# Side work queued behind the latest gate in a fused delta-rule attention and two-stage MoE kernel, with independent list scatters

## The chip, the cores and the metric

The kernel runs on one core of one Trainium2 chip. Its engines are TensorE (PE, matrix products), VectorE (DVE), ScalarE (ACT), GpSimd (POOL) and SyncE (SP, which issues most DMAs). Each engine takes its instructions strictly in the order in which the program queues them, and an instruction that waits holds all behind it on its engine. The metric is the device time of the core in microseconds (us), the median of several runs.

## What is computed

The input is q, k and v (4 batches, 8 heads, 768 positions, 48 columns) and a factor beta for each position. Three computations follow each other: a delta-rule attention, a gated feed-forward layer over the 3072 tokens with 384 columns, and a routed layer with 8 experts that gives each token to the expert with the largest logit.

```python
k_n = k / (np.linalg.norm(k, axis=-1, keepdims=True) + 1e-06)
for t in range(S):                                     # attention
    y[:, :, t] = np.einsum('bhd,bhde->bhe', q[:, :, t], state)
    v_old = np.einsum('bhde,bhd->bhe', state, kt)
    state = state + bt * np.einsum('bhd,bhe->bhde', kt, vt - v_old)
...
xn = x / rms * rms_g                                   # feed-forward
g = xn @ w_gate
x = (g / (1 + np.exp(-g)) * (xn @ w_val)) @ w_out
...
e_idx = np.argmax(x @ w_gate2, axis=1)                 # routed layer
for e in range(8):
    mask = e_idx == e
    out[mask] = gate_w * sigmoid(x @ w_og)[:, e] * (np.maximum(x[mask] @ w1[e], 0) @ w2[e])
```

(In the code of the reference the three stand as functions; the names are shortened here.)

## The kernel before

**Stages.** The sequence is cut into 6 chunks of 128 positions, m = 0 to 5, and each chunk into two groups of two batches, g = 0 and 1; (m,g) has 256 tokens. For each chunk the attention part runs `early(m)` (squares and norms of the keys with the powers nrm on GpSimd at L129, Gram products, and `solve`, the inverse of a triangular matrix in many small VectorE operations from L260 to L294, then a corner step on TensorE at L312 and L315), and for each (m,g) `late(m, g)`: a chain z (TensorE, L335), v (VectorE, L339), u (TensorE, L342), right (ScalarE, L346), y (TensorE, L357), x (ScalarE, L362), s (TensorE, L368), right (VectorE, L371), where the last hands the state to the next half. Then `scale` (L616: bss, ri, x) and `turn` (L635: the transposes xt, with xh and xl) make the operands of the feed-forward.

**The block.** `block(m, g)` (L656) is the feed-forward of one (m,g), and it is run for all 12 of them in order. It has 12 steps, called gates here and counted through the kernel from 1. One gate is 18 matmuls gv into one of two PSUM buffers (L670), tanh th and a copy of the value val on ScalarE (L676, L678), the gate multiplication on VectorE (L679), th times val on GpSimd (L681), and h with its low part on ScalarE and GpSimd (L683, L684). Two gates later TensorE multiplies h into po (L694). th and val have two buffers, h has three. "Block (1,0)" is the feed-forward of chunk 1, group 0, whose gates start with number 25.

**Weights.** The 36 pieces of the feed-forward weights come as raw tiles of 64-bit floats and are converted by hand (L508 to L614): a copy on ScalarE (L548), three steps of bit work on VectorE (L550, L551, L554), and a high and a low part on ScalarE and VectorE or GpSimd (L570, L571). The last 11 pieces share four attention buffers, so the load of one has to wait for the conversion of the one four before it.

**Routing.** After each (m,g) the router (L720 to L791) writes the numbers of its tokens into the lists of the eight experts, with two scatters of 128 tokens each, an indirect DMA that GpSimd issues (L787). The routed layer reads the lists at the end.

**The order of the work.** The class `Weave` mixes the block, as main line, with side generators: weights, lengths, early, late, scale, route and grams. Each `yield` names the TensorE time of its step and a gap until the next one, and a scheduler of the framework then orders the instructions of each engine by priority and expected times within the dependences. `issue_after(ins)` puts all instructions of a step that follow on the same engine behind ins. Before, only `solve` of chunks above 0 used it (`Attn.behind` with `M.gate`, the latest gate multiplication).

## Time and profile before

| | us |
|---|---|
| median of 3 runs | 1089.02 |
| lowest and highest run | 1082.79, 1089.41 |
| profiled execution | 1088.74 |
| its span | 1086.9 |

The trace holds each instruction's start, length, engine, source line and tiles, and for idle time what ended it. The granted clock is that of TensorE, as a share of full speed. A stretch of 100 us in which TensorE is busy for 97 has hardly any place where another engine can cost something. The trace groups instructions that follow one another into one row with a count (x4).

### The profile page before, as it was taken

To read this page: it belongs to the slowest core of one execution; us is meant where nothing else is said; L and a number is where in the kernel's file an instruction comes from. 1 tells how busy PE (TensorE), PEld (TensorE's weight loads), DVE (VectorE), ACT (ScalarE), POOL (GpSimd) and SP (SyncE) were. 2 spreads that over 40 slices of the span, in tenths; PEclk is the share of its full clock that TensorE was granted. 3 is DMA by queue.
4 is the path that set the end of the run, shared out by engine and by line. 5 is a ranking of instruction groups with operands and counts; after the bars stand their busy time and mean duration, and the time that the engine had idled before them with its cause. 6 is when DMAs were issued, how large, how long until landed. Compare 5 with 4: busy or idle time off the path is not lost.

```text
span 1086.9 us, 27674 instructions
## 1 busy us (share of the span) xinstructions
PE 976.6 (90%) x11189; PEld 918.0 (84%) x11189; DVE 698.4 (64%) x1976; ACT 474.9 (44%) x1241; POOL 460.8 (42%) x526
## 2 busy tenths in 40 slices
PE   3725888989999989999999999998998989999993
PEld 2725787889988989899989989998998989999993
DVE  5996889849963977279936975244328645557550
ACT  6625552354345434533354334434344534455440
POOL 9608343453444344444454333437533543312110
PEclk9999899999999999899999989999999999999997
DMA  9811770122212131221122120003205574345320
GB/s 290 230 59 43 220 141 1 31 75 60 45 31 64 51 65 31 46 60 45 37 70 60 31 45 17 2 17 146 73 1 167 189 249 161 111 178 200 125 87 15
DMA packets 55433, 97.05 MB, mean 89 GB/s; under 512 B 6400, under 2 KB 41878, under 8 KB 52482
## 3 DMA queue, kind: packets, MB, share of 16 engines
q1 hardware_dynamic: 45266, 48.76, 17.1%
q0 software_dynamic: 7680, 45.08, 11.9%
q8 instruction: 90, 1.47, 0.6%
q10 hardware_dynamic: 2352, 1.37, 0.5%
q14 instruction: 45, 0.37, 0.2%
HBM read 83.78 MB, written 12.09 MB: 88 GB/s over the span
## 4 chain that ended last, share of the span: by engine, by line
PE 42%; DVE 17%; issue 15%; POOL 11%; DMA 8%; ACT 5%; POOLq 0%; SPq 0%; ACTq 0%; DVEq 0%
PE gv L670 14%; PE cpo L1053 8%; PE ph L1032 7%; PE po L694 7%; DVE tmp L275 3%; POOL th L681 3%; DVE x L279 3%; POOL h L684 2%; PE y L357 2%; DVE ng L294 1%; DMA raw<-in_wv_dram 1%; POOL raw L558 1%; DMA sq<-in_kv_dram 1%; ACT h L683 1%; DVE th L679 1%
## 5 line engine op out<-in xcount | busy, mean ns | idle before, releaser
L681 POOL TENSOR_TENSOR th<-th,val 128x256 f32<-128x256 f32 x144 | 114.1, 793 | 218.7 <-DVE th L679 191.9
L694 PE MATMUL po<-wout,h 128*128 128x400 f32 x864 | 192.1, 354 | 5.5 <-ACT h L683 4.1
L683 ACT ACTIVATE h<-th 128x256 fp32r<-128x256 f32 x144 | 60.1, 417 | 231.4 <-POOL th L681 231.0
L694 PEld LDWEIGHTS po<-wout,h 128*128 128x128 f32 x864 | 148.5, 189 | 10.5 <-ACT h L683 5.3
L670 PE MATMUL gv<-xh,wl 128*128 128x256 f32 x864 | 149.2, 291 | 3.6 <-DVE th L679 3.4
L670 PE MATMUL gv<-xh,wgv 128*128 128x256 f32 x864 | 149.1, 293 | 2.5 <-DVE th L679 2.1
L679 DVE SCALAR_TENSOR_TENSOR th<-th,gv 128x256 f32<-128x256 f32 x144 | 59.8, 416 | 137.9 <-ACT val L678 134.2
L684 POOL TENSOR_TENSOR h<-th,h 128x256 fp32r<-128x256 f32 x144 | 109.5, 761 | 74.6 <-ACT h L683 74.3
L670 PEld LDWEIGHTS gv<-xh,wl 128*128 128x128 f32 x864 | 126.0, 194 | 8.1 <-DVE th L679 6.1
L670 PEld LDWEIGHTS gv<-xh,wgv 128*128 128x128 f32 x864 | 124.2, 195 | 6.3 <-DVE th L679 3.3
L1053 PE MATMUL cpo<-w2h,ch 128*128 128x384 f32 (+1 forms) x464 | 124.5, 341 | 4.6 <-ACT w2h L993 3.6
L275 DVE TENSOR_TENSOR tmp<-nb,x 128x110 f32<-128x110 f32 (+35 forms) x366 | 106.3, 330 | 3.9
L279 DVE TENSOR_TENSOR x<-x,tmp 128x110 f32<-128x110 f32 (+35 forms) x366 | 102.4, 317 | 0.2
L1032 PE MATMUL ph<-xT,w1h 128*128 128x256 f32 (+4 forms) x528 | 95.4, 315 | 0.4 <-DVE ch L1037 0.3
L1053 PEld LDWEIGHTS cpo<-w2h,ch 128*128 128x128 f32 (+1 forms) x464 | 82.0, 184 | 7.3 <-ACT w2h L993 4.3
L676 ACT ACTIVATE th<-gv 128x256 f32<-128x256 f32 x144 | 54.5, 379 | 76.9 <-PE gv L670 69.1
L1032 PEld LDWEIGHTS ph<-xT,w1h 128*128 128x128 f32 x528 | 82.9, 192 | 1.8 <-DVE ch L1037 0.6
L670 PE MATMUL gv<-xl,wgv 128*128 128x256 f32 x432 | 78.5, 288 | 0.3 <-DVE xl L651 0.2
L1053 PE MATMUL cpo<-w2l,ch 128*128 128x384 f32 (+1 forms) x232 | 78.0, 337 | 0.0
L670 PE MATMUL gv<-xl,wl 128*128 128x256 f32 x432 | 77.3, 287 | 0.0
L1037 DVE SCALAR_TENSOR_TENSOR ch<-ph,ch 128x512 fp32r<-128x512 f32 (+4 forms) x64 | 39.1, 611 | 42.8 <-ACT ch L1036 42.8
L670 PEld LDWEIGHTS gv<-xl,wgv 128*128 128x128 f32 x432 | 64.0, 195 | 1.1 <-DVE xl L651 0.7
(241 smaller groups left out, 1765.3 us busy)
## 6 DMA issues: line engine op xcount, KB each, us to landing
kT<-in_kqT_dram SPq DMA_DIRECT2D x24, 192.0 KB, 3.5
raw<-in_wo_dram SPq DMA_DIRECT2D x12, 384.0 KB, 8.0
left<-in_kqT_dram SPq DMA_DIRECT2D x24, 192.0 KB, 4.3
v<-in_kv_dram SPq DMA_DIRECT2D x12, 384.0 KB, 3.6
raw<-in_wg_dram SPq DMA_DIRECT2D x12, 384.0 KB, 3.8
raw<-in_wv_dram SPq DMA_DIRECT2D x12, 384.0 KB, 4.3
sq<-in_kv_dram SPq DMA_DIRECT2D x10, 384.0 KB, 3.5
ek<-in_kqT_dram SPq DMA_DIRECT2D x18, 192.0 KB, 3.4
```

The source lines that it names most:

```text
L275: nc.vector.tensor_tensor(out=t, in0=nb[:, k + 1:, k:k + 1].to_broadcast([P, n, b - a]), in1=x[:, k:k + 1, a:b].to_broadcast([P, n, b - a] ...
L279: nc.vector.tensor_tensor(out=x[:, k + 1:, a:b], in0=x[:, k + 1:, a:b], in1=t, op=ALU.add)
L670: nc.tensor.matmul(out=ps[:, gv], lhsT=self.weight(wi, cc, gv, slice(f * P, f * P + P)), rhs=xx[:, cc], start=i == 0, stop=i == 8)
L676: nc.scalar.activation(out=th, in_=ps[:, 0], func=AF.Tanh, scale=0.5)
L679: self.gate = nc.vector.scalar_tensor_tensor(out=th, in0=th, scalar=1.0, in1=ps[:, 0], op0=ALU.add, op1=ALU.mult).ins
L681: nc.gpsimd.tensor_tensor(out=th, in0=th, in1=val, op=ALU.mult)
L683: nc.scalar.activation(out=h2[:, 0], in_=th, func=AF.Copy)
L684: nc.gpsimd.tensor_tensor(out=h2[:, 1], in0=th, in1=h2[:, 0].bitcast(F32), op=ALU.subtract)
L694: nc.tensor.matmul(out=po[t], lhsT=h[:, ts], rhs=self.wo[wi][:, f], start=f == 0 and i == 0, stop=f == 11 and i == 2)
L1032: nc.tensor.matmul(out=ph[:, fl], lhsT=w1[wi][:, cc, f * P:(f + 1) * P], rhs=xt[:, xi, cc], start=i == 0, stop=i == 8)
L1037: nc.vector.scalar_tensor_tensor(out=hl, in0=ph, scalar=0.0, in1=hh.bitcast(F32), op0=ALU.max, op1=ALU.subtract)
L1053: nc.tensor.matmul(out=po[t][0:rows[t]], lhsT=hs[f // 2][:, hi, f % 2, t * P:t * P + rows[t]], rhs=w2[wi][:, f], start=f == 0 and i == 0, ...
```

## The change

1. The class Attn loses `due` and `behind`: the solve is no longer put behind the gate by that means.
2. `block` keeps in `evict` the latest copy of the value (ScalarE, L678) and the latest gate multiplication (VectorE, L679). `Weave.step` puts every step of every side generator behind both: all side work of ScalarE and VectorE emitted after a gate stands behind that gate's two instructions. Before the first gate `evict` is empty, and it is emptied ahead of each unit of the routed layer.
3. The list scatters are declared independent of each other, as they write slots of different tokens. The gather that reads the lists still waits for all.

```diff
-        self.due = lambda: None
...
-    def behind(self, m):
-        due = self.due() if m else None
-        return nullcontext() if due is None else self.tc.issue_after(due)
...
-        solve = self.solve(m)
-        while True:
-            with self.behind(m):
-                t = next(solve, None)
-            if t is None:
-                break
+        for t in self.solve(m):
...
-        self.ready, self.fetched, self.gate = -1, False, None
+        self.ready, self.fetched = -1, False
+        self.evict = []
...
-            nc.scalar.activation(out=val, in_=ps[:, 1], func=AF.Copy)
-            self.gate = nc.vector.scalar_tensor_tensor(out=th, in0=th, scalar=1.0, in1=ps[:, 0], op0=ALU.add,
-                                                       op1=ALU.mult).ins
+            i = nc.scalar.activation(out=val, in_=ps[:, 1], func=AF.Copy)
+            j = nc.vector.scalar_tensor_tensor(out=th, in0=th, scalar=1.0, in1=ps[:, 0], op0=ALU.add, op1=ALU.mult)
+            self.evict = [i.ins, j.ins]
...
-            nc.gpsimd.indirect_dma_start(
+            i = nc.gpsimd.indirect_dma_start(
...
-                bounds_check=NE * NT - 1, oob_is_err=False)
+                bounds_check=NE * NT - 1, oob_is_err=False).ins
+            self.tc.declare_no_dep(i, group="list", reason="slots of other tokens")
+            self.tc.add_to_no_dep_group("list", i)
...
     def step(self, side):
-        try:
-            pe, gap = next(side[0])
-        except StopIteration:
-            self.sides.remove(side)
-            return
+        with ExitStack() as st:
+            for ins in self.first():
+                st.enter_context(self.tc.issue_after(ins))
+            try:
+                pe, gap = next(side[0])
+            except StopIteration:
+                self.sides.remove(side)
+                return
...
-    A.due = lambda: M.gate
+    W.first = lambda: M.evict
...
+        M.evict = []
         W.run(C.unit(u, xg[u], xt[u], p2, new, after, next_unit, u + 1 == len(subs)))
```

No instruction is added or removed on TensorE, VectorE, ScalarE or GpSimd; what moves is their order. Line numbers after the change are some ten lower (L679 is L670, L787 is L778, L260 is L258, L275 is L273, L279 is L277, L371 is L369, L632 is L623, L129 is L127, L339 is L337).

The first place is VectorE at the first gate, whose gate multiplication writes th_1365 (raw tiles are weight pieces in conversion, nrm, n, aT and naT are norms of chunk 1, v is the chain of chunk 0). Before:

```order
L554 SCALAR_TENSOR_TENSOR raw_1610<-raw_1610 128x384
L138 RECIPROCAL n_1418<-n_1418 128x32
L551 SCALAR_TENSOR_TENSOR raw_1569<-raw_1569 128x384
L571 TENSOR_TENSOR wgv_82<-raw_1124,wgv_81 128x384
L139 TENSOR_TENSOR n_1418<-n_1418,beta 128x32
L554 SCALAR_TENSOR_TENSOR raw_1569<-raw_1569 128x384
L141 STREAM_TRANSPOSE aT_1422<-n_1418 128x32
L571 TENSOR_TENSOR wl_1607<-raw_1550,wl_1607 128x384
L143 TENSOR_SCALAR naT_1424<-aT_1422 128x32
L679 SCALAR_TENSOR_TENSOR th_1365<-th_1365,gv_1278 128x256
```

And now:

```order
L369 TENSOR_TENSOR right_78<-right_78,s_1052 48x8x48 x2
L545 SCALAR_TENSOR_TENSOR raw_1124<-raw_1124 128x384
L369 TENSOR_TENSOR right_79<-right_79,s_1085 48x8x48 x2
L562 TENSOR_TENSOR wgv_82<-raw_1124,wgv_81 128x384
L337 TENSOR_TENSOR v_0_802<-v_0_802,z_1104 128x4x48
L337 TENSOR_TENSOR v_0_802<-v_0_802,z_1105 128x4x48
L670 SCALAR_TENSOR_TENSOR th_1365<-th_1365,gv_1278 128x256
L541 TENSOR_SCALAR raw_1217<-raw_1217 128x384
L541 TENSOR_SCALAR raw_1399<-raw_1399 128x384
L133 TENSOR_SCALAR nrm_1232<-nrm_1232 128x32
L541 TENSOR_SCALAR raw_1407<-raw_1407 128x384
```

The conversions of the later pieces and the norms of chunk 1 stand behind the first gate now; the gate itself moved from row 229 of VectorE's order to row 177. The first transpose of the solve of chunk 1 (L260) moved from behind the fifth gate to behind the ninth, and the first of the transposes at its end (L288) from behind gate 16 to behind gate 21.

The second place is VectorE at the 24th gate (th_3099), the last of block (0,1), with the scale of (1,0) (bss_3024 and x_2582) and the solve of chunk 2 (tmp and x_3003). Before:

```order
L279 TENSOR_TENSOR x_3003<-x_3003,tmp_2_3042 128x29x2
L371 TENSOR_TENSOR right_78<-right_78,s_2984 48x8x48 x2
L625 TENSOR_SCALAR bss_3024<-bss_3024 128x2
L245 TENSOR_TENSOR left_77<-gq_3068,maskU 64x4x128 x2
L632 SCALAR_TENSOR_TENSOR x_2582<-x_2582,ri_3088,rmsg 128x384 x2
L679 SCALAR_TENSOR_TENSOR th_3099<-th_3099,gv_3047 128x256
L275 TENSOR_TENSOR tmp_3_3108<-nb_2927,x_3003 128x56 x2
```

And now, 41 rows behind that gate:

```order
L277 TENSOR_TENSOR x_3003<-x_3003,tmp_8_3202 128x23x5
L273 TENSOR_TENSOR tmp_9_3253<-nb_2927,x_3003 128x110 x2
L277 TENSOR_TENSOR x_3003<-x_3003,tmp_9_3253 128x22x5 x2
L369 TENSOR_TENSOR right_78<-right_78,s_2984 48x8x48 x2
L273 TENSOR_TENSOR tmp_10_3258<-nb_2927,x_3003 128x105
L616 TENSOR_SCALAR bss_3024<-bss_3024 128x2
L716 TENSOR_SCALAR y_3235<-po_2147 128x384
L273 TENSOR_TENSOR tmp_10_3258<-nb_2927,x_3003 128x126
L277 TENSOR_TENSOR x_3003<-x_3003,tmp_10_3258 128x21x5
L277 TENSOR_TENSOR x_3003<-x_3003,tmp_10_3258 128x21x6
L623 SCALAR_TENSOR_TENSOR x_2582<-x_2582,ri_3088,rmsg 128x384 x2
```

The scale of (1,0) stood ahead of the 24th gate and of the rows of the solve from tmp_3 on; now it stands behind the gate and behind tmp_0 to tmp_10.

The third place is GpSimd at gates 39 to 42, with the two scatters of the routing of pos_4436 and the powers nrm of chunk 3. Before:

```order
L681 TENSOR_TENSOR th_4173<-th_4173,val_4175 128x256
L787 DMA list<-tok,pos_4436 25600x1
L684 TENSOR_TENSOR h_4179<-th_4173,h_4179 128x256
L787 DMA list<-tok,pos_4436 25600x1
L681 TENSOR_TENSOR th_4255<-th_4255,val_4257 128x256
L684 TENSOR_TENSOR h_4261<-th_4255,h_4261 128x256
L681 TENSOR_TENSOR th_4336<-th_4336,val_4338 128x256
L684 TENSOR_TENSOR h_4342<-th_4336,h_4342 128x256
L129 TENSOR_TENSOR nrm_4349<-ss_4348,half 128x8 x2
L681 TENSOR_TENSOR th_4460<-th_4460,val_4462 128x256
```

And now:

```order
L672 TENSOR_TENSOR th_4173<-th_4173,val_4175 128x256
L675 TENSOR_TENSOR h_4179<-th_4173,h_4179 128x256
L672 TENSOR_TENSOR th_4255<-th_4255,val_4257 128x256
L675 TENSOR_TENSOR h_4261<-th_4255,h_4261 128x256
L672 TENSOR_TENSOR th_4336<-th_4336,val_4338 128x256
L127 TENSOR_TENSOR nrm_4349<-ss_4348,half 128x8
L675 TENSOR_TENSOR h_4342<-th_4336,h_4342 128x256
L778 DMA list<-tok,pos_4436 25600x1 x2
L127 TENSOR_TENSOR nrm_4349<-ss_4348,half 128x8 x3
L672 TENSOR_TENSOR th_4460<-th_4460,val_4462 128x256
```

The scatters moved two gates later and stand side by side; the four powers, of which two stood four gates earlier, stand around them. At gates 64 and 88 four powers stand directly ahead of the pair.

## Rows read from the trace of the kernel before

**Rows 1.** The head of the page: span, and busy time of TensorE.

```profile
span 1086.9 us, 27674 instructions
...
PE 976.6 (90%) x11189; PEld 918.0 (84%) x11189; DVE 698.4 (64%) x1976; ACT 474.9 (44%) x1241; POOL 460.8 (42%) x526
```

**Rows 2.** Windows: start:end, length, busy per engine (instructions), clock, DMA share, GB/s.

```profile
100.00:150.00 50.00, 45.32 (x600) 40.96 (x598) 41.62 (x85) 33.93 (x88) 23.05 (x20) 0.90 0.80 199
...
250.00:350.00 100.00, 97.32 (x1386) 89.59 (x1386) 69.92 (x225) 43.23 (x121) 43.96 (x52) 1.00 0.19 45
```

**Rows 3.** Windows of the solve of chunk 1 and the chain behind it.

```profile
158.60:206.70 48.10, 43.67 (x290) 40.02 (x290) 45.32 (x168) 14.04 (x43) 20.33 (x25) 0.96 0.04 9
206.70:254.50 47.80, 43.05 (x898) 39.96 (x899) 28.74 (x60) 24.73 (x64) 22.25 (x23) 0.96 0.27 69
```

**Rows 4.** The list of waits: who waited for whom, us in total, times, longest.

```profile
POOL list L787 <- DMA list<-tok,pos: 24.5, 8, 4.6
...
PE y L357 <- ACT right L346: 10.9, 8, 2.6
```

**Rows 5.** Timeline of GpSimd: start, us, line, operation, count [idle before <-what ended it].

```profile
440.09 1.06 POOL L787 DMA_INDIRECT list<-tok,pos  x1 [0.17 <-issue]
445.77 0.98 POOL L787 DMA_INDIRECT list<-tok,pos  x1 [4.62 <-DMA list<-tok,pos]
446.76 0.77 POOL L681 TENSOR_TENSOR th<-th,val 128x256 f32<-128x256 f32 x1
447.46 3.29 POOL L129 TENSOR_TENSOR nrm<-ss,half 128x8 f32<-128x8 f32 x2
```

**Rows 6.** Timeline of VectorE at the first gates.

```profile
132.49 0.42 DVE L679 SCALAR_TENSOR_TENSOR th<-th,gv 128x256 f32<-128x256 f32 x1 [1.45 <-ACT val L678]
...
138.07 1.09 DVE L551 SCALAR_TENSOR_TENSOR raw<-raw 128x384 int32<-128x384 int32 x1
```

**Rows 7.** Timeline of VectorE from the solve of chunk 1 to the scale.

```profile
158.61 2.07 DVE L260 STREAM_TRANSPOSE nb<-xr 128x1024 f32<-128x1024 f32 x1
...
173.11 0.41 DVE L679 SCALAR_TENSOR_TENSOR th<-th,gv 128x256 f32<-128x256 f32 x1
...
204.84 1.99 DVE L288 STREAM_TRANSPOSE ng<-xa 128x1024 f32<-128x1024 f32 x1
...
237.20 0.57 DVE L339 TENSOR_TENSOR v<-v,z 128x192 f32<-128x192 f32 x2
...
242.98 0.20 DVE L275 TENSOR_TENSOR tmp<-nb,x 128x31 f32<-128x31 f32 x1
...
246.78 1.11 DVE L371 TENSOR_TENSOR right<-right,s 48x384 f32<-48x384 f32 x2
```

**Rows 8.** Timeline of TensorE: first matmul of the first block and of block (1,0).

```profile
119.76 1.65 PE L670 MATMUL gv<-xh,wgv 128*128 128x256 f32 x6
...
254.53 0.88 PE L670 MATMUL gv<-xh,wgv 128*128 128x256 f32 x6
```

**Rows 9.** Timeline of TensorE: the five y that waited behind a list scatter.

```profile
396.31 0.32 PE L357 MATMUL y<-right,left 128*64 128x48 f32 x2 [2.62 <-ACT right L346]
...
451.00 1.02 PE L357 MATMUL y<-right,left 128*64 128x48 f32 x8 [2.13 <-ACT right L346]
...
567.68 1.54 PE L357 MATMUL y<-right,left 128*64 128x48 f32 x17 [1.05 <-ACT right L346]
...
630.86 0.45 PE L357 MATMUL y<-right,left 128*64 128x48 f32 x2 [2.63 <-ACT right L346]
...
733.80 0.32 PE L357 MATMUL y<-right,left 128*64 128x48 f32 x2 [0.67 <-ACT right L346]
```

**Rows 10.** Windows of 10 us behind three of them: the clock is third from the right.

```profile
390.00:400.00 10.00, 7.34 (x89) 6.69 (x90) 5.91 (x25) 3.83 (x11) 5.60 (x7) 0.90 0.40 53
...
450.00:460.00 10.00, 8.91 (x142) 7.82 (x143) 2.38 (x8) 6.93 (x21) 2.89 (x4) 0.66 0.07 14
...
630.00:640.00 10.00, 9.14 (x94) 8.50 (x95) 4.39 (x16) 5.52 (x17) 5.20 (x7) 0.66 0.22 51
```

More of the change, by code (lines that the diff above doesn't have):

```diff
@@ L1162, with __init__ @@
 class Weave:
-    def __init__(self):
-        self.t, self.sides = 0.0, []
+    def __init__(self, tc):
+        self.tc, self.t, self.sides = tc, 0.0, []
+        self.first = lambda: []
     def add(self, gen, wait=0.0):
@@ L1222, in tile_kernel @@
     M = Moe1(tc, bw, work, ps, c, a)
-    W = Weave()
+    W = Weave(tc)
     scales = {}
```

## The prediction

> **What bounds the kernel now.** I read the head of the page first: TensorE is busy in 976.6 us of a span of 1086.9 [rows 1]. The profiled execution took 1088.74 us, so 1.84 us lie around the span; the median of the runs shown is 1089.02, 0.28 above it. All sums below start from 1088.74.
>
> Busy time by stretch says where TensorE is not full. Between 100 and 150 us it works 45.32 of 50, between 250 and 350 us 97.32 of 100 [rows 2]; in the latter kind of stretch the change can return only a few single stalls. In the two stretches that hold the solve of chunk 1 and the chain behind it TensorE works 43.67 of 48.10 and 43.05 of 47.80 [rows 3]. In the first of these VectorE works 45.32 of 48.10: the solve is a string of small VectorE operations, and VectorE is its limit. In the second VectorE works 28.74 of 47.80 and nothing is full: it is a chain over all engines. So I read the front (up to the first matmul of block (1,0) at 254.53 [rows 8]) as a chain, and the rest as TensorE's work plus stalls.
>
> The list of waits names the stalls that the last part of the change is about: GpSimd stands 24.5 us, in 8 pieces of up to 4.6, at a list scatter until another has landed, and TensorE stands 10.9 us in 8 pieces at y for ScalarE's copy right [rows 4]. One place shows how they hang together: a scatter at 440.09, the next at 445.77 after 4.62 us of waiting, and only then GpSimd's th work [rows 5]. ScalarE's copy h needs that th, right is issued on ScalarE behind h, and TensorE's y at 451.00 waited 2.13 us for right [rows 9].
>
> **Part 1, the start.** No operation is added or removed on any compute engine, so nothing is paid for instructions; only places move. In the order of VectorE 52 rows fewer stand ahead of the first gate, most of them weight conversions. Before, the first gate ran at 132.49 [rows 6] although its first matmul was issued at 119.76 [rows 8]. In the changed order the rows ahead of it are those of the weights that its own matmuls need, so I let it run as soon as its 18 matmuls and the copy are done, at some 121 to 122: 11 us earlier. That gain is not kept whole. The moved conversions make the later weight pieces, a step of which takes up to 1.09 us [rows 6], and in the order of SP the fetches of the last pieces (raw) now stand behind loads that wait for y and s of chunk 0. I let 3.5 us of the 11 be lost by the ninth gate (bounds: none, and all 11).
>
> The solve of chunk 1 begins on VectorE at 158.61, behind the fifth gate. In the changed order it begins behind the ninth. The ninth gate ran at 173.11 [rows 7]; 173.11 - 11 + 3.5 = 165.6, and the first operation of the solve follows at once. So the solve starts 165.6 - 158.6 = **7.0 us later** (bounds 3.5 and 14.5). Its length up to the end of the transpose that started at 204.84 is 204.84 + 1.99 - 158.61 = 48.2 us. I keep that, since VectorE is its limit and about as many other operations stand in it as before. Its end moves from 206.8 to 213.8.
>
> **Part 2, from the solve to block (1,0).** Before, 254.53 - 206.83 = 47.7 us pass from there to the first matmul of block (1,0): corner, chain of chunk 1 for both groups, scale. TensorE fills it with gates 16 to 24 [rows 3]. In the changed order the solve ends behind gate 21 and the chain's matmuls stand together behind the 24th, with little block work left to put between. For that the chain itself is shorter: its matmuls no longer queue behind gv. Against it stand operations that come ahead of the scale of (1,0) on VectorE: 28 solve operations of chunk 2 all stand there now, where ten did (the other 18 stood behind the scale). The ten took 246.78 - 242.98 = 3.8 us [rows 7], so 28 take some 10.6. But from v at 237.20 to the copy right at 246.78 the chain went for 9.6 us through u, right, y, x and s on other engines [rows 7], so nearly all of the 10.6 lies beside those, and 1 to 2 us come out. I take 46 us for the 47.7: 3.2 less for the matmuls that are gone from between, 1.5 more for the rows. Bounds: 29, if VectorE's own 28.74 us of work [rows 3] were all that is left of the chain, and 52, if the rows hold the chain by half of their length more.
>
> Block (1,0) then starts at 213.8 + 46 = 259.8 against 254.53: **+5.3 us**. The bounds together give 210.3 + 29 = 239 and 221.3 + 52 = 273, so -15 to +19. From there on each engine's order is within half a gate of the one before, apart from GpSimd's, and TensorE is full, so the shift is carried to the end.
>
> **Part 3, the scatters.** In the order of GpSimd the pair of scatters is now a group of two, with no th or h between and no wait between them. One takes 1.06 us of GpSimd [rows 5]. The five places where the wait reached TensorE are y rows that waited 2.62, 2.13, 1.05, 2.63 and 0.67 us [rows 9]: 9.1 us. Behind three of them the granted clock fell, to 0.90 in 390 to 400 and to 0.66 in 450 to 460 and 630 to 640 [rows 10]. A mean of 0.66 over 10 us is work for 6.6, so 3.4 us each, and 1.0 for the first: 7.8 us. Together **16.9 us** come back at most, if y no longer waits.
>
> It will not all come back. At three of the pairs (gates 41, 64 and 88) the four powers nrm of the next chunk now stand in one block with the pair, where two stood by it before and two some gates earlier. Two powers took 3.29 us [rows 5], so the th behind the block waits 2 x 1.06 + 3 x 1.65 = 7.1 us at gate 41 (one power is ahead of an h) and 8.7 at the others. Before, th waited 5.68 + 0.98 = 6.7 us from the first scatter to the end of the second [rows 5]. At those three a stall like the old one may stay. I take 30% of the gain back: 16.9 - 5.0 = **-12 us** (bounds 0 and -16.9).
>
> The Trainium skill (DMA: Bandwidth & Descriptors, section "Anatomy of one DMA — SWDGE (gpsimd) path") gives about 2.0 us as the fixed cost of a DMA issued from GpSimd. By it the second scatter would wait about 1 us, and the pairs would be worth a third of the above: an estimate of -4, and 1090 in all. The trace disagrees: with 4.62 us of waiting it took 5.68 us from scatter to scatter [rows 5], and the measured waits decide.
>
> **The sum.** 1088.74 + 5.3 - 12 = 1082.0.
>
> **Rivals.**
> 1. *The front gains.* If TensorE, and not the chain, sets the pace up to block (1,0), the 11 us of the earlier first gate count nearly whole: block (1,0) at some 245, -9.5, and with the lists at -13 this gives 1066. For it: TensorE works 43.67 + 43.05 = 86.7 of the 95.9 us around the solve [rows 3], so moving its work earlier must empty some place. Against it: the solve is VectorE's, and it starts four gates later.
> 2. *The list waits do not turn into gain.* Scatters and powers in one block hold th as long as the wait did, or y then waits for something else, and the front costs its 5.3: 1088.74 + 5.3 - 2 = 1092. For it: the 7.1 and 8.7 against 6.7 us above. Against it: nine of the twelve pairs have no powers behind them. That the change does nothing would give 1089; the order shows every pair moved, so I add no chance for that.
> 3. *Slower: side work held back at the start.* The ring of raw tiles is refilled only behind gates, so the conversions end late, and the solve of chunk 1 starts at 172, not 165.6. The chain then stands almost alone on TensorE, with the clock as low in parts of it as the 0.66 behind a stall of 2 us [rows 10], for 3 to 5 us more. Block (1,0) starts at 172 + 48.2 + 49 + 4 = 273, +19; with the lists at -5 this is 1103. It decides from a start of block (1,0) at some 270 on. For it: the first solve operation waits in order behind all conversions that now follow the gates. Against it: only the last 11 of 36 pieces share the ring.
>
> **How the numbers follow.** About 1% (11 us: 1078 and 1100) is what a measurement can tell from no change here. The forecast has 0.45, with its own range 1072 to 1090; a third of it lies below 1078. Rival 1 has 0.22, all below 1078. Rival 2 has 0.17, all within 1%. Rival 3 has 0.16, all above 1100. Faster: 0.15 + 0.22 = 0.37. Same: 0.30 + 0.17 = 0.47. Slower: 0.16. The range from 1064 to 1101 leaves out most of rival 3 and a small part of rival 1, together under 0.2.
>
> **What would show it.** Part 1: the first gate at 121 to 122, the ninth near 165, the solve's first transpose at 165 to 166. Part 2: the solve's transpose ends near 214 and block (1,0) has its first matmul at 258 to 262; a start at 247 or less is rival 1, one behind 268 is rival 3. Part 3: no wait of a list scatter for another in the list of waits, TensorE's waits at y for right under 5 us where they were 10.9, and the clock at 1.00 in the stretch that answers to 450 to 460; if they stay near 10, it is rival 2. The prediction fails if a stall appears that stands in no row here, above all at the weights of the first four gates.

## The result, and the profile after

The changed kernel takes 1104.31 us (median of 4 runs, 1100.9 to 1104.33), the kernel before on the same chip 1088.2 (4 runs): a ratio of 1.015, 95% interval 1.011 to 1.019. It is slower by 1.5%, where 1082.0 and a likeliest outcome of no clear difference stood in the prediction. The third rival came, with 1103. The profiled execution took 1104.3 us, against 1088.74.

The head of the page of the changed kernel, as in [rows 1]:

```profile
span 1102.5 us, 27688 instructions
...
PE 982.8 (89%) x11189; PEld 923.1 (84%) x11189; DVE 707.7 (64%) x1976; ACT 477.2 (43%) x1241; POOL 458.4 (42%) x526
```

TensorE is busy 6.2 us longer for the same 11189 matmuls, and the span is 15.6 longer. Windows of the changed kernel (columns as in [rows 2]): a fixed stretch, then its own solve and chain, which answer to [rows 3].

```profile
100.00:150.00 50.00, 40.45 (x530) 35.50 (x528) 36.51 (x74) 28.10 (x75) 18.22 (x17) 0.90 0.62 177
173.90:221.60 47.70, 41.72 (x290) 38.23 (x289) 46.91 (x166) 13.37 (x41) 21.59 (x26) 1.00 0.04 10
221.60:272.50 50.90, 39.81 (x790) 35.78 (x788) 32.46 (x81) 21.34 (x52) 13.17 (x13) 0.69 0.26 64
```

The solve is as long as before (47.7 us). The chain behind it takes 50.9 us where it took 47.8, and its granted clock is 0.69 where it was 0.96: TensorE works 39.81 of 50.90 us there, and on fewer matmuls (790 where there were 898). Between 100 and 150 TensorE also does less than before.

VectorE's timeline of the changed kernel, from the first gate to gate 25, the first of block (1,0) (columns as in [rows 5]):

```profile
122.43 0.42 DVE L670 SCALAR_TENSOR_TENSOR th<-th,gv 128x256 f32<-128x256 f32 x1 [5.32 <-ACT val L669]
...
166.92 0.41 DVE L670 SCALAR_TENSOR_TENSOR th<-th,gv 128x256 f32<-128x256 f32 x1
...
167.72 2.10 DVE L562 TENSOR_TENSOR wl<-raw,wl 128x384 fp32r<-128x384 f32 x2
...
173.94 2.01 DVE L258 STREAM_TRANSPOSE nb<-xr 128x1024 f32<-128x1024 f32 x1 [2.85 <-DMA xr<-kk]
...
219.53 2.06 DVE L286 STREAM_TRANSPOSE ng<-xa 128x1024 f32<-128x1024 f32 x1
...
278.26 0.42 DVE L670 SCALAR_TENSOR_TENSOR th<-th,gv 128x256 f32<-128x256 f32 x1 [5.34 <-ACT val L669]
```

The first gate is 10.1 us earlier than in [rows 6], the ninth 6.2 earlier than in [rows 7], the first transpose of the solve 15.3 later. TensorE's timeline has the start of block (1,0):

```profile
272.46 1.65 PE L661 MATMUL gv<-xh,wgv 128*128 128x256 f32 x6
```

That is 17.9 us later than in [rows 8]. Counting the gate multiplications in both traces gives the account of the span: gate 29 comes at 294.0 where it came at 276.5 (+17.5), gate 144, the last, at 818.0 where it came at 805.6 (+12.4). So the front loses 17.5 us, the blocks win back 5.1, and 3.2 more are lost behind the last gate. (One trace each; in a trace of the unchanged kernel on another chip, the control below, gate 29 came 3.1 us later and gate 144 7.1 us later, so terms of 3 us are not safe: against that trace the blocks win back 9.1 us.)

The list of waits of the changed kernel, as in [rows 4]:

```profile
PE gv L661 <- DVE th L670: 9.8, 9, 2.6
...
PE u L340 <- DVE v L337: 5.0, 3, 3.3
...
PE gk L215 <- DMA ek<-in_kqT_dram: 4.3, 5, 1.9
...
PE y L355 <- ACT right L344: 2.1, 2, 1.3
```

No scatter waits for a scatter any more, and y waits 2.1 us for right where it waited 10.9. Other waits have grown: gv for th from 5.5 to 9.8, u for v from 1.4 to 5.0, gk for the load ek from 2.5 to 4.3.

### The profile page after: what moved, and what is told of

Its sections match the earlier page's. It is cut to its first block, busy times and chain, and to the rows that moved or that the text cites. A ratio compares the mean times of both kernels' runs of the same rounds, so it can differ in the third digit from the quotient of the medians.

```text
span 1102.5 us, 27688 instructions
## 1 busy us (share of the span) xinstructions
PE 982.8 (89%) x11189; PEld 923.1 (84%) x11189; DVE 707.7 (64%) x1976; ACT 477.2 (43%) x1241; POOL 458.4 (42%) x526
## 4 chain that ended last, share of the span: by engine, by line
PE 58%; DVE 13%; issue 10%; DMA 7%; POOL 6%; ACT 3%; SPq 0%; POOLq 0%; DVEq 0%; ACTq 0%
PE gv L661 22%; PE po L685 10%; PE cpo L1047 8%; PE ph L1026 7%; DVE tmp L273 2%; DMA sq<-in_kv_dram 2%; DVE x L277 2%; PE y L355 2%; PE gq L236 2%; PE s L366 1%; PE off L313 1%; PE z L333 1%; POOL nrm L127 1%; PE u L340 1%; POOL raw L549 1%
## 5 line engine op out<-in xcount | busy, mean ns | idle before, releaser
L670 DVE SCALAR_TENSOR_TENSOR th<-th,gv 128x256 f32<-128x256 f32 x144 | 59.9, 416 | 183.8 <-ACT val L669 172.3
L661 PEld LDWEIGHTS gv<-xh,wl 128*128 128x128 f32 x864 | 125.7, 194 | 10.9 <-DVE th L670 8.7
L273 DVE TENSOR_TENSOR tmp<-nb,x 128x110 f32<-128x110 f32 (+35 forms) x366 | 108.3, 335 | 3.8
L277 DVE TENSOR_TENSOR x<-x,tmp 128x110 f32<-128x110 f32 (+35 forms) x366 | 99.6, 310 | 0.3
L661 PE MATMUL gv<-xl,wgv 128*128 128x256 f32 x432 | 80.9, 293 | 1.2 <-DVE xl L642 1.2
```

Source lines behind the costliest of these rows:

```text
L273: nc.vector.tensor_tensor(out=t, in0=nb[:, k + 1:, k:k + 1].to_broadcast([P, n, b - a]), in1=x[:, k:k + 1, a:b].to_broadcast([P, n, b - a] ...
L277: nc.vector.tensor_tensor(out=x[:, k + 1:, a:b], in0=x[:, k + 1:, a:b], in1=t, op=ALU.add)
L661: nc.tensor.matmul(out=ps[:, gv], lhsT=self.weight(wi, cc, gv, slice(f * P, f * P + P)), rhs=xx[:, cc], start=i == 0, stop=i == 8)
L670: j = nc.vector.scalar_tensor_tensor(out=th, in0=th, scalar=1.0, in1=ps[:, 0], op0=ALU.add, op1=ALU.mult)
```

## The experiments

Chips differ: the kernel before had medians of 1088.2, 1101.87, 1094.88, 1101.76, 1104.17 and 1092.59 us on those used here. So each run is read by its ratio to the kernel before on the same chip. Gate times come from one trace each.

The theory after the result had two parts. The front pays for queueing the weight conversions behind gates, since they end late and the solve waits for them; and the lists gain what Part 3 said, only less of it. The rivals: the front pays for other queued work; the y stalls vanish through the queueing and not through the independence; the queueing costs everywhere.

**The lists alone.** The kernel before with the independence of the scatters and nothing else:

```diff
-            nc.gpsimd.indirect_dma_start(
+            i = nc.gpsimd.indirect_dma_start(
...
+            self.tc.declare_no_dep(i, group="list", reason="slots of other tokens")
+            self.tc.add_to_no_dep_group("list", i)
```

> The kernel before with the list scatters independent of each other and nothing else. Theory (the scatters' wait reaches TensorE at y, 9.1 us of stalls and some of the 7.8 us of clock behind them): 8 to 12 us faster than before, some 1078, no wait of a list scatter for another, and y waits for right under 4 us. Rival (the waits are hidden or come back elsewhere): 1086 to 1090.

Measured: 1109.76 against 1101.87, 1.0066 (1.0038 to 1.0094). A gain of about 1% was forecast, and it is a small loss. The list wait is gone and y waits 1.7 us, so the mechanism worked; but its list of waits has these rows:

```profile
ACT sq L107 <- DMA sq<-in_kv_dram: 23.9, 10, 7.5
...
PE gk L217 <- DMA ek<-in_kqT_dram: 7.2, 5, 4.9
```

In a trace of the unchanged kernel (the control below) they are 15.1 and 3.3; and TensorE's wait for the first gathered rows (xg) of the routed layer is 5.9 us, where the control has 2.2. Up to 728 us the order on TensorE, VectorE and ScalarE is that of before but for some 14 rows. Behind that it differs, so the total is not the scatters' alone. One place shows their part. GpSimd's timeline of this run, then SP's (which issues the load), then TensorE's:

```profile
322.73 1.07 POOL L787 DMA_INDIRECT list<-tok,pos  x1 [0.72 <-DVE run L775]
324.10 0.98 POOL L787 DMA_INDIRECT list<-tok,pos  x1 [0.30 <-issue]
```

```profile
325.97 0.85 SPq L204 DMA_DIRECT2D ek<-in_kqT_dram  x2
```

```profile
334.88 0.47 PE L217 MATMUL gk<-ek 48*64 48x64 f32 x2 [4.91 <-DMA ek<-in_kqT_dram]
```

and the windows of that stretch:

```profile
326.00:328.00 2.00, 2.00 (x18) 2.00 (x19) 0.00 (x0) 1.57 (x3) 0.84 (x2) 1.00 0.13 37
...
330.00:332.00 2.00, 0.00 (x0) 0.00 (x0) 0.35 (x1) 0.00 (x0) 0.35 (x1) 1.00 0.19 22
332.00:334.00 2.00, 0.00 (x0) 0.00 (x0) 0.00 (x0) 0.00 (x0) 0.00 (x0) 1.00 0.76 200
```

A load issued 2 us behind a pair of scatters was used 8.9 us after its issue. The DMA engines were busy for 13 to 21% of the time between 326 and 332 and for 76% only after that, and from 332 to 334 every engine stood still. In the control one scatter ran at 326.21, the load went out at 329.00, the second scatter ran at 331.54, and gk started at 333.88, 4.9 us behind its load, having waited 0.90 us. SP's and TensorE's timelines of the control:

```profile
329.00 0.85 SPq L204 DMA_DIRECT2D ek<-in_kqT_dram  x2
```

```profile
333.88 0.33 PE L217 MATMUL gk<-ek 48*64 48x64 f32 x2 [0.90 <-DMA ek<-in_kqT_dram]
```

Loads issued just behind a scatter land late. The traces have the landing of most loads: in the changed kernel, between 200 and 740 us, the ten that SP issued within 2 us of the start of a list scatter landed 4.3 to 9.2 us after their issue (median 7.6), 95 others after a median of 3.3; six of the ten are loads of one kind (left), with a median of 7.4, where the eight others of that kind have 3.9. Behind a scatter that goes alone it is less but not nothing: a median of 4.4 against 3.1 in the trace of before (five such loads), 6.5 against 3.2 in the second run with split pairs below (four). What inside the DMA path does it is not shown.

**The queue alone, and the control.** The changed kernel with dependent scatters (the two lines of the diff that declare the independence removed), and the kernel before unchanged, for a trace.

> The changed kernel with the list scatters dependent as before, so the queueing alone. Theory (the queueing costs 17 us up to block (1,0) and some 6 at the entry of the routed layer, and the scatters give 8 back): 1110 to 1114. Rival (the scatters give nothing in this order, since powers and scatters stand in one block): 1103 to 1106, as the changed kernel. The first gate of block (1,0) at 278 in both.

Measured: 1122.42 against 1101.87, 1.0182 (1.0125 to 1.0239), gate 29 at 299.6; y waits 2.1 us. The whole change has 1.015 (1.011 to 1.019) on another chip, so by the times the independence is worth 0.3%, which the intervals do not tell from nothing or from 1%. By the traces it does something in the front: gate 29 came at 294.0 and 295.0 in the two kernels with everything queued and independent scatters (the second is the run with the last block free below), and at 299.6 and 300.5 in the two with dependent ones (the second is the run with the front alone queued).

> The kernel before, unchanged, for a trace on the same chip as the others: the same time as before. If the chip is the slower one of the first four experiments (some 1102 instead of 1088), the trace shows where that lies; theory: in the routed layer, behind gate 144, since the first four experiments lie 8 to 14 us farther behind at the end than they did at gate 140, against the trace of before.

Measured: 1096.45 against a median of 1094.88. In its trace scatters wait 30.8 us for scatters and y 8.7 for right.

**The queue in parts: place.** Queueing only from block (1,0) on, with the solve ordered as before until then; once with independent lists and once with dependent ones. Against the changed kernel:

```diff
-    W.first = lambda: M.evict
+    W.first = lambda: M.evict if M.on else []
+    A.due = lambda: None if M.on or not M.evict else M.evict[1]
...
+            M.on = M.on or (m, g) == (1, 0)
             W.run(M.block(m, g, hook))
```

> The changed kernel, with the queueing switched on only where block (1,0) begins; until there the order is that of before (the solve behind the latest gate, nothing else). Scatters independent. Theory (the loss up to block (1,0) is from the side work queued in the first 24 gates): first gate of block (1,0) at 260 to 262, total 1080 to 1087, depending on whether the 6 us at the entry of the routed layer stay. Rival (the queueing costs through the blocks as well): above 1095.

Measured: 1096.39 against 1101.87, 0.9957 (0.9924 to 0.999); gate 29 at 276.0, as before. The whole loss sits in the front.

> The kernel that queues side work from block (1,0) on, with the list scatters dependent as before. Theory (the scatters alone cost 7 us in the order of before but pay with the queueing): 8 to 12 us slower than the same kernel with independent scatters, so ratio 1.003 to 1.010 to before. Rival (it is the queueing that gains the 4 to 5 us and the scatters do nothing): ratio 0.993 to 0.998.

Measured: 1089.08 against 1094.88, 0.9951 (0.9918 to 0.9985). The same with the list dependence as without. Its list of waits:

```profile
POOL list L786 <- DMA list<-tok,pos: 32.5, 11, 7.6
...
PE y L356 <- ACT right L345: 2.1, 4, 1.1
```

GpSimd waits at the scatters for 32.5 us, as long as ever, and y hardly waits, here as in the queue alone above. So what takes the y stalls away in the changed kernel is that side work is queued, not that the scatters are independent.

The opposite, queueing in the first two blocks only, with dependent lists (`M.on = m == 0` in the place of the line above):

> The kernel before with side work queued behind the latest gate and copy in the first two blocks (gates 1 to 24) only, then the order of before; list scatters dependent as before. Theory (the front is the loss): gate 28 some 18 to 23 us later than before, ratio 1.015 to 1.022. Rival (the loss is in the blocks or at the entry of the routed layer): ratio under 1.010.

Measured: 1117.74 against 1094.88, 1.0224 (1.0144 to 1.0304); gate 29 at 300.5, the first transpose of the solve at 173.51. The front alone costs more than the whole change. With dependent scatters throughout, front and rest give 1.0224 x 0.9951 = 1.017, beside 1.0182 measured for the queue alone: the two places add up.

**The queue in parts: whose work.** The changed kernel with the weight generator exempt, and the kernel before with the weight generator alone queued (the edit of the first is shown):

```diff
-            for ins in self.first():
+            for ins in () if side in self.free else self.first():
...
-    W.add(weigh(), WSTART)
+    W.free.append(W.add(weigh(), WSTART))
```

> The changed kernel, with the weight generator alone exempt from the queueing; all other side work queued as in the changed kernel. Scatters independent. Theory (the solve of chunk 1 is late because conversions of weights stand behind gates and ahead of it on VectorE): the solve's first transpose at 157 to 161, first gate of block (1,0) at 258 to 265, total 1085 to 1092. Rival (what delays the chain is the other side work, queued behind gates on ScalarE and VectorE): first gate of block (1,0) stays at 272 or later, total 1098 or more.

Measured: 1108.42 against 1101.87, 1.0048 (1.0018 to 1.0078). The last conversion ends at 149.8. VectorE's timeline and TensorE's:

```profile
161.35 2.06 DVE L258 STREAM_TRANSPOSE nb<-xr 128x1024 f32<-128x1024 f32 x1
```

```profile
229.21 0.42 PE L215 MATMUL gk<-ek 48*64 48x64 f32 x4 [2.85 <-DMA ek<-in_kqT_dram]
```

The solve starts 2.7 us later than before and ends on time at 207.6, but gate 29 is still 9.2 us late. The chain behind the solve has the gap at gk, and its windows show a low clock (two stretches, then the whole chain):

```profile
207.60:213.00 5.40, 2.72 (x130) 2.40 (x130) 5.37 (x5) 0.81 (x2) 1.05 (x2) 0.95 0.01 3
213.00:228.00 15.00, 12.93 (x191) 12.15 (x191) 3.71 (x14) 6.05 (x12) 7.30 (x7) 0.56 0.39 79
...
207.62:263.93 56.31, 49.80 (x898) 46.45 (x899) 29.81 (x67) 25.12 (x64) 23.72 (x24) 0.82 0.27 65
```

TensorE works 2.72 of the 5.40 us behind the solve, and the next 15 us run at 0.56 (in the kernel before 3.84 and then 0.95, in the run queued from (1,0) 4.49 and then 0.95). Over the chain it does the same 898 matmuls as before in 49.80 us of work instead of 43.05 [rows 3]: 6.8 of the 8.5 us that the chain is longer are slower work, and the rest is idle time. One trace suggests what starts it: ScalarE's copy w of the corner step ran at 212.51, behind an h that had waited 5.13 us for GpSimd's th, where in the run queued from (1,0) the first piece of w ran at 208.99, ahead of that h.

> The kernel before with the weight generator alone queued behind the latest gate and copy; list scatters dependent, everything else as before. Theory (the conversions behind gates hold up the solve of chunk 1): the solve's first transpose at 172 to 175, first gate of block (1,0) 15 to 20 us later than before, ratio 1.014 to 1.020. Rival (the loss needs the other side work queued too): ratio 1.003 to 1.010.

Measured: 1114.42 against 1101.76, 1.0113 (1.0064 to 1.0163); gate 29 at 290.5 (+14.0). VectorE's timeline:

```profile
169.65 1.08 DVE L570 TENSOR_TENSOR wl<-raw,wl 128x384 fp32r<-128x384 f32 x1 [0.30 <-ACT wl L569]
...
173.01 2.10 DVE L259 STREAM_TRANSPOSE nb<-xr 128x1024 f32<-128x1024 f32 x1 [1.02 <-ACT xr L222]
```

and the window of its chain, from the end of the solve to block (1,0):

```profile
220.50:269.05 48.55, 39.06 (x810) 35.67 (x809) 31.88 (x97) 22.47 (x57) 14.41 (x14) 0.75 0.31 76
```

The weights alone delay the solve as the whole change does. With the run before: of the front's 2.2% the conversions make about 1.1, and the other queued work about 0.9 (1.0048 against 0.9957).

**The queue in parts: which engine.** Queueing from block (1,0) on behind the gate multiplication alone (VectorE), and behind the copy of the value alone (ScalarE), with dependent lists:

```diff
+            self.pair = [j.ins]          # or [i.ins]
...
-    W.first = lambda: M.evict if M.on else []
+    W.first = lambda: M.pair if M.on and M.evict else []
```

> Side work queued from block (1,0) on, on VectorE behind the gate multiplication only; list scatters dependent. Theory (the gain of 0.5% comes from the gate multiplication standing ahead of side work on VectorE, which frees gv and feeds GpSimd's th earlier): ratio 0.993 to 0.997. Rival (it comes from ScalarE's copy): ratio 0.999 to 1.002.

> Side work queued from block (1,0) on, on ScalarE behind the copy of the value only; on VectorE only the solve behind the gate, as before; list scatters dependent. Theory (VectorE brings the gain): ratio 0.998 to 1.002, TensorE's waits at y for right stay at 8 to 11 us. Rival (ScalarE brings it): ratio 0.993 to 0.997 and those waits under 3 us.

Measured against 1101.76: VectorE 1101.41, 1.0003 (0.9969 to 1.0038), y waits 2.3 us; ScalarE 1107.03, 1.0042 (1.0018 to 1.0067), y waits 14.8. So it is VectorE's queue that frees y, and with y freed the time stayed where it was. Neither alone gains, and both together gave 0.995 (on another chip; the intervals of 0.995 and 1.0003 just overlap). Why is open.

**The end.** The wait of the first gather's rows (xg) at the entry of the routed layer is 5.5 us in the changed kernel and 1.9 before. Two runs take the last block's side work out of the queue, one from the changed kernel, one from the kernel queued from (1,0):

```diff
+            if (m, g) == (NM - 1, 0):
+                W.first = lambda: []
```

> The changed kernel with the queueing switched off in the last block (5,1), which is followed by the routed layer. Theory (the routing of the last block comes late behind the gates, the write of its rows is late, and the gather xg of the first unit behind it): 4 to 6 us faster than the changed kernel, ratio 1.009 to 1.012 to before, and TensorE's wait for xg under 2 us. Rival (the 5.5 us wait there only shows work that was moved): ratio as the changed kernel, 1.015.

> Side work queued from block (1,0) up to block (5,0), the last block free; scatters dependent, in pairs. If the late routing of the last block costs 3 us at the entry of the routed layer: ratio 0.990 to 0.993, TensorE's wait for xg under 2.5 us. If the wait for xg there (5.3 us in the queued kernel) only takes the place of other time: 0.994 to 0.997.

Measured: 1107.06 against 1094.88, 1.0124 (1.0046 to 1.0202), xg 2.6 us; and 1098.13 against 1104.17, 0.9958 (0.9937 to 0.9979), xg 1.5. The first overlaps 1.015 and decides nothing; the second equals the kernels without the edit. The wait shrinks, and no gain in time is measured.

**What the scatters cost.** The kernel before without the 24 scatters (the lists stay empty, so the routed layer gathers no listed tokens), and with the first of each pair only (half of the tokens are not listed):

```diff
-        for t in range(2):
+        for t in range(1):
```

> The kernel before without the 24 list scatters (the lists stay empty, so the routed layer gathers only the padding row; its work is the same size). It bounds what scatters can cost. Theory of the prediction (waits at scatters reach TensorE, 16.9 us with the clock): ratio 0.984 to 0.988. Theory now (the wait at the second scatter was mostly cover, since the side work moves up to the next limit): ratio 0.993 to 1.002.

Measured: 1069.08 against 1101.76, 0.9718 (0.9658 to 0.9778). Gate 144 comes at 780.3, 25.3 us earlier than in the trace of before (on another chip), so most of the gain is in the blocks and not in the routed layer, which had less to read. That is more than the 16.9 us of stalls and clock that Part 3 counted.

> The kernel before with the first scatter of each pair alone: the other half of the tokens is not listed, the routed layer's work keeps its size. No scatter has another ahead of it to wait for. Theory A (the cost is the wait of the second for the first): nearly the whole 2.8% of the kernel without scatters, ratio 0.972 to 0.979. Theory B (each scatter costs by itself): half of it, ratio 0.983 to 0.989.

Measured: 1082.43 against 1104.17, 0.9817 (0.9777 to 0.9857). The second scatter of each pair costs 1.8%, the first about 1.0, as the two stand in the kernel before.

**The pair split.** The kernel before with dependent scatters, the second one held back behind a later th of GpSimd (`self.mul`), some two gates on, so that the first has landed:

```diff
-            nc.gpsimd.tensor_tensor(out=th, in0=th, in1=val, op=ALU.mult)
+            self.mul = nc.gpsimd.tensor_tensor(out=th, in0=th, in1=val, op=ALU.mult).ins
...
         for t in range(2):
-            nc.gpsimd.indirect_dma_start(
+            with self.tc.issue_after(self.mul) if t else nullcontext():
+                nc.gpsimd.indirect_dma_start(
...
-            yield 0, 3.0
+            yield 0, 3.0 if t else 9.0
```

> The kernel before with the second scatter of each pair queued behind a th that is about two gates later on GpSimd; dependent as before, so that it finds the first landed. Theory A (the wait is the cost): the list of waits holds under 5 us for scatters where it had 24.5 to 31, TensorE's waits at y for right under 4 us, ratio 0.980 to 0.990. Theory B (each scatter costs by itself): ratio 0.996 to 1.004, as each of the two now holds up GpSimd and the loads in a place of its own.

Measured: 1091.65 against 1104.17, 0.9892 (0.9855 to 0.9929). Its waits:

```profile
PE gk L217 <- DMA ek<-in_kqT_dram: 4.4, 6, 1.4
...
POOL list L788 <- DMA list<-tok,pos: 2.1, 1, 2.1
PE y L357 <- ACT right L346: 2.1, 3, 1.2
```

Both waits are gone, as with independent scatters, and the engines wait little longer for the loads than in the control: ek 4.4 us, sq 16.7. The edit moves hardly anything else: the order of VectorE is that of before, that of ScalarE differs by one row and that of TensorE by four. A gain of the 12 us that Part 3 forecast is there, by another edit. Whether it comes through y is not shown, since VectorE's queue freed y as well and gained nothing; the split also frees GpSimd of its wait.

> The kernel before with the pairs split by two gates, as e14. Ratio 0.986 to 0.993 if the gain is firm; 0.996 to 1.0 if e14's four runs were lucky.

Measured on another chip: 1080.33 against 1092.59, 0.9878 (0.985 to 0.9905); scatters wait 2.7 us once, y 2.2. The same gain twice: this is the fastest kernel with the whole output, 1.2% under the kernel before and, by the ratios, 2.7% under the changed one.

> The same split of the pairs, with side work queued behind gate and copy from block (1,0) on. By theory A and the gain of the queueing from (1,0): ratio 0.980 to 0.990. By theory B: 0.993 to 0.998, as the queueing from (1,0) alone (0.995).

> Pairs split by two gates, side work queued behind gate and copy from block (1,0) up to block (5,0), the last block free. If the gains add and only the entry of the routed layer ate them: ratio 0.982 to 0.988, TensorE's wait for xg at the entry under 3 us. If in the queued order the wait at the scatter was already covered: 0.993 to 0.997.

Split pairs with the queue from (1,0): 1096.5 against 1104.17, 0.9945 (0.9922 to 0.9968), and with the last block free 1083.2 against 1092.59, 0.992 (0.9891 to 0.9949). The queue adds no gain to the split. Both take the same y stalls away. In one trace each on the same chip, the kernel with both is 3.3 us ahead at gate 144 (797.9 against 801.2) and takes 298.8 us from there to the end, where the split alone takes 289.0; with the last block free that stretch is as long as with the split alone (281.9 against 283.4), and the time is still no better.

## Why the prediction was wrong, step by step

**Part 1, first half: right.** The first gate was forecast at 121 to 122 and came at 122.43, the ninth at about 165 and came at 166.92.

**Part 1, "the first operation of the solve follows at once": the step that failed first.** The solve was set to start at 165.6 and started at 173.94, outside its bound of 14.5 us later. Two things stand between the ninth gate and the solve. The last raw tiles' conversions follow the gate (167.72, for 2.10 us), where before the last of them had ended at 151.8:

```profile
151.25 0.54 DVE L571 TENSOR_TENSOR wl<-raw,wl 128x384 fp32r<-128x384 f32 x1
```

And the solve's own input is fetched after that. The tile views of raw (by SP) and of xr in the changed kernel (issues, durations in ns, first and last start):

```profile
L528 SPq DMA_DIRECT2D raw<-in_wv_dram x4: 328/355/382, 140.8 to 161.0; - x4
```

```profile
L390 SPq DMA_DIRECT2D xr<-kk x4: 328/414/420, 168.8 to 170.7; - x4
```

The same two views of the kernel before:

```profile
L537 SPq DMA_DIRECT2D raw<-in_wv_dram x4: 327/350/412, 118.7 to 132.4; - x4
```

```profile
L396 SPq DMA_DIRECT2D xr<-kk x4: 419/420/430, 152.2 to 153.6; - x4
```

The last raw tile was requested at 161.0, where before it was at 132.4, and xr at 168.8 to 170.7, where it was at 152.2 to 153.6. The four buffers of the ring are those in which the solve of chunk 1 then works. So its input can be fetched only when a conversion has freed one, each conversion now waits for a gate, and each raw tile waits for the conversion four before it. I had this ring as rival 3 and dismissed it with "only the last 11 of 36 pieces share the ring": 11 pieces, each a round behind gates, were enough. The run with the weights alone queued shows it (173.01, and +14.0 us at gate 29), and the run with them exempt (161.35).

**The solve's length: right.** 48.2 us kept; 47.65 measured (173.94 to 221.59).

**Part 2, the chain: wrong in sign.** Forecast 46 us, "its matmuls no longer queue behind gv"; measured 50.9, within the bound of 52. The kernel before has 47.7, and 13 runs here whose side work is not queued in the front have 47.8 to 50.0. The gv did leave the chain (790 matmuls where there were 898), but they had kept TensorE working. In the solve it worked 41.72 of 47.70 us at a clock of 1.00; in the chain behind it, with those gates already done, 39.81 of 50.90 at 0.69. So it stood idle for 11.1 us, where [rows 3] has 4.8, and for much of the time it did its work at the lower of the two levels (1.2 of 2.4 GHz). Two waits make 6.7 of the 11.1 us (TensorE's timeline):

```profile
244.55 1.67 PE L685 MATMUL po<-wout,h 128*128 128x400 f32 x4 [3.39 <-ACT h L674]
...
256.65 0.63 PE L340 MATMUL u<-v,ng 64*64 64x48 f32 x7 [3.35 <-DVE v L337]
```

The h came late because its th stood on GpSimd behind two powers nrm (240.13 to 243.36). The v came late because VectorE had the first two operations of the solve of chunk 2 ahead of it (253.08 to 256.2). The prediction put 1.5 us on such rows, since they lay beside work of other engines; these two did not. The run with the weights alone queued has the same late chain, 810 matmuls, 9.5 us idle and a clock of 0.75, and takes 48.6 us: no gain there either. Of the low clock the prediction knew the rows (0.66 behind stalls, [rows 10]) and used them only in rival 3.

The weights are not all of it. With them exempt the solve was nearly on time and gate 29 still 9.2 us late, mostly by slower work (0.56 behind the solve, 0.82 over the chain). Other side work queued behind gates, which the chain needs, is a cause of about equal size; the trace points to the copy w of the corner step, and no run separated it.

So the start of block (1,0), forecast at 259.8, came at 272.46: above the mark of 270 from which rival 3 decides, and within 1 us of the 273 worked out there. Rival 3 was given 0.16. Its mechanism was right, and that its sum of 1103 was right too is in part luck: its solve started 1.9 us too early, its chain was 2.1 us too long, its 5 us for the lists came from the queue, and the 3.2 us behind the last gate were not in it. Its condition was to be read from the ring's buffers, not argued from the count of its pieces.

**Part 3, the scatters: a gain of that size exists, but not by this edit.** The blocks won back 5.1 us (9.1 against the control), where 12 was forecast. TensorE's windows behind the former stalls read as forecast:

```profile
450.00:460.00 10.00, 10.00 (x195) 9.61 (x189) 3.33 (x14) 6.66 (x15) 3.75 (x6) 1.00 0.07 19
630.00:640.00 10.00, 10.00 (x125) 9.31 (x124) 8.01 (x33) 3.11 (x10) 4.31 (x6) 1.00 0.01 2
```

The clock is 1.00 there, where it was 0.66 [rows 10], and y hardly waits. But this is the queue's doing. Independence alone took the wait from GpSimd and gave it to the loads behind the pair: beside the control y waits 7.0 us less, but TensorE waits 3.9 us more at gk and 3.7 more at xg, and ScalarE 8.8 more at sq. In the changed kernel the loads behind a pair land late too, but gk waits 4.3 us, hardly more than the 3.8 with dependent scatters. Splitting the pair, which leaves the dependence, gained 1.1 to 1.2%.

The doubt about blocks of powers and scatters was looked at in the wrong place. GpSimd's timeline of the changed kernel at gate 41:

```profile
349.32 1.06 POOL L778 DMA_INDIRECT list<-tok,pos  x1 [0.17 <-issue]
350.68 0.98 POOL L778 DMA_INDIRECT list<-tok,pos  x1 [0.30 <-issue]
351.67 4.88 POOL L127 TENSOR_TENSOR nrm<-ss,half 128x8 f32<-128x8 f32 x3
356.52 0.73 POOL L672 TENSOR_TENSOR th<-th,val 128x256 f32<-128x256 f32 x1
```

From 349.32 to 356.52 are 7.2 us, as the 7.1 forecast, and yet y does not wait there, since right is no longer behind that h. ScalarE's timeline:

```profile
354.78 1.38 ACT L344 ACTIVATE right<-u 64x192 f32<-64x192 f32 x4
359.77 0.42 ACT L674 ACTIVATE h<-th 128x256 fp32r<-128x256 f32 x1
```

The order sets whether a late th reaches y, not how late the th is.

On the two microseconds of fixed cost for a DMA issued from GpSimd (the Trainium skill, DMA: Bandwidth & Descriptors, section "Anatomy of one DMA — SWDGE (gpsimd) path") the traces still disagree: the list scatters between 254 and 830 us landed 3.4 to 10.1 us after their issue before the change, median 4.8, and 4.4 to 8.9 after it, median 6.0 (18 and 14 scatters whose landing the traces hold). By the medians a pair in flight together lands later than one at a time.

**The sum.** +5.3 for the front was +17.5, -12 for the blocks was -5.1, and nothing behind the last gate was +3.2: together +15.6 for a forecast of -6.7.

**What stays open.** Which queued work beside the weights makes the front late; through what the split pairs gain; why the queue from (1,0) gains only with both engines in it; how much of a scatter's 1% to 1.8% per kernel is GpSimd's time and how much the loads that it holds up; and the 3.2 us behind the last gate, which may be chance between traces.

## What to carry to other kernels

Before side work is put behind the main line, list the buffers it holds and who needs them next: a ring that is refilled only in the main line's rhythm finishes late, and here the next critical stage worked in that ring's buffers. Matmuls that fill the gaps of a chain on the path are not in its way: when they were moved ahead of it here, idle time and a lower clock took their place. And a wait that is removed must be followed to the transfers that then meet: to space two DMAs apart gained 1.1 to 1.2%, to let them go together cost 0.7% by itself and gained nothing measurable with the queue.

## What the runs showed of the hardware

Two scatters of 128 tokens issued within 1.4 us from GpSimd went with a delay of plain loads that another engine issued 2 us later: 8.9 us from issue to use instead of 4.9, with the DMA engines busy for 13 to 21% of the time at first. In the changed kernel ten loads issued within 2 us of the start of a scatter landed after a median of 7.6 us, 95 others after 3.3. Without the 24 scatters, which take 1.05 us of GpSimd each, the kernel is 2.8% shorter, some 31 us. And a stretch in which TensorE was busy for 39.81 of 50.90 us had a granted clock of 0.69, while [rows 3] has 0.96 with 43.05 of 47.80. With the weights exempt the same 898 matmuls took 49.80 us of work at 0.82.
